# Attention and MLP block on one core: whole products and five exp banks in the half cycles after the last max product

## The chip, the cores and the metric

The kernel runs on one core of a Trainium2 chip. The metric is the device time of one execution in microseconds (us), the median of several runs. A profile of one execution is read beside it. The engines are called as in the profile: PE (TensorE, the matmul array; PEld is its weight load), DVE (VectorE), ACT (ScalarE), POOL (GpSimd), SP (SyncE, which issues the transfers).

## What is computed

One block with an adaptive layer norm: attention with 32 query heads of width 16 over one shared key and value head, then a two-layer MLP, on 2048 rows of width 512, in float32.

```python
mod = (_silu(c) @ w_mod).reshape(c.shape[0], 6, 1, -1)
sa, ca, ga, sb, cb, gb = (mod[:, 0], ..., mod[:, 5])
h = _layernorm(x, axis=-1) * (1 + ca) + sa
q = (h @ wq).reshape(B, S, 32, 16).transpose(0, 2, 1, 3)
k, v = h @ wk, h @ wv
p = _softmax(jnp.einsum("bhqd,bkd->bhqk", q, k) * 16 ** -0.5)
x = x + ga * (jnp.einsum("bhqk,bkd->bhqd", p, v) ... @ wo)
h = _layernorm(x, axis=-1) * (1 + cb) + sb
x = x + gb * (_gelu(h @ w1 + b1) @ w2 + b2)
```

## The kernel before

Products are made in float32 accuracy out of two rounded parts: each operand is split into a high and a low part, and one product becomes three (high x high, low x high, high x low).

**Units, steps, half cycles.** The queries are cut in eight blocks of 256 rows; a unit is one block with four heads, so there are 64 units (`units`, line 462), and eight steps in each (`steps`, line 1305), a step being two key tiles of 128. The main loop (lines 1350 to 1448) takes two steps at a time, X = K and Y = K + 1, and does them as two half cycles. A half cycle issues, on PE:

- four **exp products** (`sexp`, line 590), scores of a key tile against a unit's queries. They contract only 64 rows, so two of them, called s = 0 and s = 1, lie on the two halves of the array. Each fills a PSUM bank named e; ACT reads the bank with an exp (line 611) into the tile p.
- **max products** (`Max.step`, line 498, banks of tag m): the same scores in another order for a unit several units ahead; DVE reduces each to a maximum (line 510), which is later put in as a row of the queries by `put_max` (POOL line 553, SP line 548). They run ahead, so they end before the loop does. The last unit's last max product belongs to the first pair of steps of the last unit but one.
- a **batch** of the MLP's or a projection's products (`take`, line 1169; the lists come from `batches`, line 167). Such products contract 128 rows. In the loop each is done as two halves of 64 rows (`half`, line 187; `halves`, line 1374): the first half beside exp products on the other half of the array, the second in the next half cycle.
- the **pv step** (`pv`, line 619, line 628): the exps of an earlier half cycle times the values, summed in acc.

**Banks.** PSUM has three e banks, three of tag m, one each of tags x and v. `sexp` takes the e banks in turn from the list `banks` (line 586).

**Order.** The order of the instructions on every engine is that in which the program issues them; `issue` (line 1320) merges lists of products by their lengths. When a batch is there, `beside` and `follow` hold the exp of one exp product back until another, of the other half of the array, has been issued. Delayed work is put in a list with `later`, counted in ticks of `clock`, four to a pair of steps; each tick of the tail takes one batch.

**The end.** While the last block is in attention, the MLP of the block before it (number 6) is in its second product, w2: two tiles of 33 products each (`rest_steps`, lines 1015 to 1027). The batch of the first tile is `BATCH - 1` = 5 long, of the second 6; `batches` counts them from the end, so that the first batch is the short one. What isn't issued when the loop ends is issued whole (`whole`, line 179, line 181) in the tail, lines 1452 to 1466. There the last block's rest runs with `fast`: 18 products wops, then `TAIL[0]` = 4 ticks, six products wops that need the last unit's normalised result (onH, onL), `TAIL[1]` = 8 ticks, then transposes tp, w1 and w2 of the last block.

Of the kernel before, what the change touches and what calls it, by code (L numbers as in the profile page):

```python
# [8 lines left out]
F32 = mybir.dt.float32  # L9
# [5 lines left out]
P = 128  # L15
# [18 lines left out]
BATCH = 6  # L34
# [16 lines left out]
def adaln_mqa_mlp(  # L51
# [99 lines left out]
    def due():  # L151
        now = [p for p in pending if p[0] <= clock[0]]
        pending[:] = [p for p in pending if p[0] > clock[0]]
        for _, fn in now:
            fn()
# [11 lines left out]
    def batches(ps, pairs, size, ready=lambda n: True, begin=True, end=True):  # L167

        todo = [(a, b_) for wh, wl, xh, xl in pairs for a, b_ in ((wh, xh), (wl, xh), (wh, xl))]
        last = len(todo) - 1  # L170

        ends = list(range(len(todo), 0, -size))[::-1]
        for begin_, end_ in zip([0] + ends, ends):
            part = range(begin_, end_)
            while not ready(part[-1] // 3):
                yield -1
            yield [(ps, *todo[n], begin and n == 0, end and n == last) for n in part]

    def whole(batch):
        for ps, a, b_, first_, last_ in batch:  # L180
            nc.tensor.matmul(ps, a, b_, start=first_, stop=last_)  # L181
# [408 lines left out]
    def sexp(u, K, j, s, line=None):  # L590

        w = blocks[units[u][0]][1]
        qst = qsts[u]
        assert u in placed
        n = u * steps[0] + K
        if n < 3 and n not in pbufs:
            pbufs[n] = att.tile([P, 2, 2, 512], F32, name=f"p{n}", tag="p", bufs=3)
        pt = pbufs[n % 3]
        bank = banks.pop(0)
        banks.append(bank)  # L600
        e = psum.tile([P, 512], F32, name=f"e{u}_{K}_{j}_{s}", tag=f"e{bank}", bufs=1)
        rows = slice(64 * s, 64 * s + 64)
        if w == 512:
            kt, rhs = K, qst[rows, j, :]
        else:
            kt, rhs = 2 * K + j, qst[rows].rearrange("p j n -> p (j n)")
        nc.tensor.matmul(e, ks[rows, kt * P:(kt + 1) * P], rhs, start=True, stop=True)  # L607
        dst = pt[:, j, s, :]

        def exp():  # L610
            ins = nc.scalar.activation(dst, e, AF.Exp, scale=0.25)  # L611
            for old in written.pop((n - 3, j, s), ()):
                tc.declare_no_dep(ins.ins, old, reason="the products that read the tile's last contents come between the two")
            written.setdefault((n, j, s), []).append(ins.ins.name)
            return ins

        return exp() if line is None else line.append(exp)
# [190 lines left out]
    def rest_steps(b, fast, rp, bank, ons, ready):  # L808
# [4 lines left out]
        for hf in range(w // HQ):  # L813
# [201 lines left out]
            for t in range(2):  # L1015
                sl = slice(t * P, (t + 1) * P)
                for cols in (slice(0, D), ):
                    place = dict(tag="m", bufs=3) if b == len(blocks) - 2 and t else bank()
                    ps = psum.tile([P, D], F32, name=f"w2ps{b}_{hf}_{t}_{cols.start}", **place)
                    ops = [(gH[:, f, sl], gL[:, f, sl], w2H[:, f, cols], w2L[:, f, cols]) for f in range(NF)]  # L1020
                    size_ = BATCH - 1 if b == len(blocks) - 2 and not t else BATCH
                    yield from batches(ps[:, :cols.stop - cols.start], ops, size_, lambda f: made.issuperset(range(f + 1)))
                    if fast:
                        later(1, lambda t=t, ps=ps, cols=cols: store(t, ps, cols))
                        yield 2
                    else:
                        store(t, ps)
# [126 lines left out]
    def resume():  # L1154

        go_on(holder[0])
# [190 lines left out]

    keep_warm(WARM[3], tag="e2", bufs=1)
    behind = None
    for u in range(NU):  # L1350
        for K in range(0, steps[u], 2):
            goal = lead[u] + (lead[u + 1] - lead[u]) * (K + 2) / steps[u]
            goal = min(goal, first[u + QBUFS] if u + QBUFS < NU else first[NU])
            n = max(0, 2 * round((goal - mp.done) / 2))

            def maxes(s, n, first_=1.0, held=None):
                return [(1.0 if i else first_, lambda i=i: mp.step(s, held if i >= 2 else None)) if mp.has(s) else (0.0, lambda: None)
                        for i in range(n)]

            def exps(s, which):  # L1360
                return [(1.0, lambda K=K, j=j: sexp(u, K, j, s)) for K, j in which]

            def beside(s, which):

                K, j = which[-1]
                return exps(s, which[:-1]) + [(1.0, lambda: sexp(u, K, j, s, waiting))]

            def follow(s, K, j):

                state["witness"] = sexp(u, K, j, s)  # L1370
                while waiting:
                    waiting.pop()()

            def halves(batch, s):

                ahead = (SHORT if short else AHEAD) / products(batch)
                behind_ = None if s == 0 and batch[0][3] else state["witness"]
                return [(ahead * products([one]), lambda i=i, one=one: half(one, s, None if i else behind_))
                        for i, one in enumerate(batch)]

            def plain(s, K, t, n):

                one, other = maxes(s, n), maxes(t, n)
                if not holder and mp.has(t) and n > 1:

                    other[0] = 1.0, lambda: mp.step(t, tag="x", bufs=1)
                issue(mixture(exps(s, [(K, 0), (K, 1)]), one), exps(t, [(K, 0)]) + other + exps(t, [(K, 1)]))

            X, Y = K, K + 1

            due()
            batch = take() if behind else None
            short = batch and products(batch) < SHORT + 0.01
            if short:
                issue(mixture(maxes(1, n // 2), exps(1, [(X, 0), (X, 1)])),
                      exps(0, [(X, 0)]) + halves(batch, 0) + [(1.0, lambda: follow(0, X, 1))])
            elif batch:
                groups = [mixture(maxes(1, n // 2, 0.01), beside(1, [(X, 0), (X, 1), (Y, 0)])),  # L1400
                          halves(batch, 0) + [(1.0, lambda: follow(0, X, 0))]]
                issue(*(reversed(groups) if batch[0][3] else groups))
            else:
                plain(1, X, 0, (n + 2) // 4)
            clock[0] += 1
            due()
            if behind:
                end_step(*behind)
            clock[0] += 1
            due()  # L1410
            if batch:

                reduces, gone = [], []

                def hold(reduce):
                    reduce() if gone else reduces.append(reduce)

                def go_on_():
                    resume()
                    gone.append(True)  # L1420
                    while reduces:
                        reduces.pop(0)()

                hold = hold if batch[-1][4] else None

                if short:
                    issue(mixture(maxes(0, n // 2, held=hold), exps(0, [(Y, 0), (Y, 1)])),
                          exps(1, [(Y, 0)]) + halves(batch, 1) + [(0.0, go_on_), (1.0, lambda: follow(1, Y, 1))])
                else:
                    issue(mixture(maxes(0, n // 2, 0.01, hold), beside(0, [(X, 1), (Y, 0), (Y, 1)])),  # L1430
                          halves(batch, 1) + [(0.0, go_on_), (1.0, lambda: follow(1, Y, 1))])
                advance()
            else:
                plain(1, Y, 0, n // 4)
            clock[0] += 1
            due()
            end_step(u, X)
            behind = (u, Y)
            clock[0] += 1
            if state["mods"] and state["q"] == 0 and w2H is None:  # L1440
                w2H = att.tile([P, NF, D], F32R, name="w2H", tag="bigH")
                w2L = att.tile([P, NF, D], F32R, name="w2L", tag="bigL")
                preps["w2"] = prep_w2()
            if clock[0] >= prepared[0] + PREP and weights and weights[0] in preps and not state["busy"]:
                prepared[0] = clock[0]
                for _ in range(state["turns"]):
                    if weights and next(preps[weights[0]], 0) == 0:
                        weights.pop(0)
# [51 lines left out]
```

## Time and profile before

| | us |
|---|---|
| median of 3 runs | 1564.13 (1564.03 to 1564.39) |
| span of the profiled execution | 1563.1 |
| busy: PE | 1546.5 |
| busy: DVE | 1401.7 |
| busy: ACT | 1228.8 |
| busy: POOL | 681.7 |

The span runs from the first instruction to the last of the profiled execution; its own time is that span, and the runs' median is 1.0 us longer. Busy time of PE counts an array that has any product in flight as busy, even if only one half of it is used, and the ends of products are modelled. So PE's share says little about how well it is filled: the starts of products, seen in the timeline, say more. "64*128" in a row is the part of the array in use (rows x columns), 64x512 the operand. A bracket behind a row is the idle time of the engine before it and what ended it.

### The profile page before, as it was taken

The page shows a single profiled execution, that of the slowest core. Times are in us where ns is not written, and L with a number is a line of the kernel's source. Part 1 is how long each engine was busy: PE and PEld are TensorE (multiplying, and loading weights), DVE is VectorE, ACT ScalarE, POOL GpSimd, SP SyncE. Part 2 cuts the span into 40 slices and gives each one's busy share as a digit, 9 for nine tenths or more (in the row PEclk, how much of TensorE's full clock was granted, in tenths as well). Part 3 has the DMA queues.
Part 4 walks back from the last instruction along what each step waited for, and adds up shares of the span by engine and source line. Part 5 has one row for each costly group of instructions (what it writes and reads, how often), then busy time and mean ns, then how long its engine had stood idle before and what let it go on. Part 6 is the DMA issues. An engine that isn't in the chain of part 4 may idle for free.

```text
span 1563.1 us, 41433 instructions
## 1 busy us (share of the span) xinstructions
PE 1546.5 (99%) x16387; PEld 959.9 (61%) x16387; DVE 1401.7 (90%) x2479; ACT 1228.8 (79%) x2392; POOL 681.7 (44%) x1194
## 2 busy tenths in 40 slices
PE   7999999999999999999999999999999999999999
PEld 4455555567655665557655675556655676556667
DVE  7999999999999999999999999999999999999625
ACT  5577778788777887788877887788877888788853
POOL 5545433877323570246422472245611573235711
PEclk9999999999999999999999999999999999999999
DMA  7235412313030211213022120303112130312241
GB/s 244 97 96 194 152 52 89 120 52 97 19 110 19 83 60 35 93 29 99 29 62 69 57 84 26 105 16 97 43 50 79 46 97 20 102 34 66 81 150 61
DMA packets 83126, 121.63 MB, mean 78 GB/s; under 512 B 19614, under 2 KB 56222, under 8 KB 82676
## 3 DMA queue, kind: packets, MB, share of 16 engines
q1 hardware_dynamic: 82916, 118.97, 23.5%
q8 instruction: 130, 2.13, 0.6%
q14 instruction: 64, 0.52, 0.1%
q10 hardware_dynamic: 16, 0.00, 0.0%
HBM read 91.13 MB, written 27.27 MB: 76 GB/s over the span
## 4 chain that ended last, share of the span: by engine, by line
PE 84%; DVE 10%; issue 3%; POOL 2%; DMA 1%; ACT 0%; ACTq 0%; SPq 0%; POOLq 0%; DVEq 0%
PE acc L628 28%; PE m L505 24%; PE e L607 16%; DVE mx L510 8%; PE w1ps L191 8%; PE w2ps L181 2%; PE w2ps L191 1%; PE w1ps L181 1%; DMA xt<-in_A_x_dram 1%; PE qps L191 1%; PE tp L191 1%; PE wops L191 1%; PE kps L162 1%; DVE st L835 1%; DVE x L828 1%
## 5 line engine op out<-in xcount | busy, mean ns | idle before, releaser
L510 DVE TENSOR_REDUCE mx<-m 128x1 f32<-128x512 f32 x2048 | 1270.5, 682 | 86.9 <-PE m L505 63.8
L611 ACT ACTIVATE p<-e 128x512 f32<-128x512 f32 x2048 | 1099.3, 598 | 257.4 <-PE e L607 110.5
L505 PE MATMUL m<-ks,qst 64*128 64x512 f32 x2048 | 832.4, 429 | 1.9 <-DVE mx L510 0.6
L607 PE MATMUL e<-qst,ks 64*128 64x512 f32 x2048 | 747.6, 412 | 0.1
L628 PE MATMUL acc<-p,va 128*32 128x256 f32 x8192 | 548.0, 385 | 0.0
L505 PEld LDWEIGHTS m<-ks,qst 64*128 64x128 f32 x2048 | 366.5, 184 | 212.3 <-DVE mx L510 174.8
L607 PEld LDWEIGHTS e<-qst,ks 64*128 64x128 f32 x2048 | 362.5, 184 | 95.2 <-ACT p L611 71.1
L628 PEld LDWEIGHTS acc<-p,va 128*32 128x32 f32 x8192 | 213.7, 109 | 213.1 <-issue 110.0
L553 POOL TENSOR_SCALAR mt<-turned 8x32 f32<-8x32 f32 x256 | 53.1, 208 | 418.9 <-DVE turned L559 406.9
L191 PE MATMUL w1ps<-h2H,w1t 64*128 64x256 f32 x1232 | 235.6, 287 | 0.0
L191 PEld LDWEIGHTS w1ps<-h2H,w1t 64*128 64x128 f32 x1232 | 185.8, 184 | 28.9 <-DVE mx L510 17.7
L191 PE MATMUL w1ps<-h2L,w1t 64*128 64x256 f32 x616 | 169.2, 275 | 0.0
L191 PE MATMUL w2ps<-w2H,gH 64*128 64x512 f32 x284 | 123.8, 436 | 0.0
L191 PEld LDWEIGHTS w1ps<-h2L,w1t 64*128 64x128 f32 x616 | 114.0, 185 | 0.0
L191 PE MATMUL w2ps<-w2L,gH 64*128 64x512 f32 x282 | 110.9, 393 | 0.0
L191 PE MATMUL w2ps<-w2H,gL 64*128 64x512 f32 x282 | 110.2, 391 | 0.0
L954 POOL TENSOR_SCALAR tt<-tt 128x256 f32<-128x256 f32 x77 | 31.0, 403 | 142.6 <-ACT tt L953 109.3
L137 POOL TENSOR_TENSOR gL<-z,gH 128x256 fp32r<-128x256 f32 x77 | 57.0, 740 | 6.4
L955 POOL TENSOR_TENSOR tt<-tt,z 128x256 f32<-128x256 f32 x77 | 56.7, 736 | 6.4
L965 POOL TENSOR_TENSOR z<-tt,z 128x256 f32<-128x256 f32 x77 | 56.4, 733 | 6.0
L964 POOL TENSOR_TENSOR tt<-tt,z 128x256 f32<-128x256 f32 x77 | 56.4, 732 | 0.0
L191 PEld LDWEIGHTS w2ps<-w2H,gL 64*128 64x128 f32 x282 | 52.2, 185 | 0.4
(190 smaller groups left out, 1480.9 us busy)
## 6 DMA issues: line engine op xcount, KB each, us to landing
w1t<-dw SPq DMA_DIRECT2D x82, 512.0 KB
qst<-dq SPq DMA_DIRECT2D x384, 32.0 KB
do<-oc SPq DMA_DIRECT2D x64, 128.0 KB
dw<-w1s SPq DMA_DIRECT2D x11, 512.0 KB
xt<-in_A_x_dram SPq DMA_DIRECT2D x4, 1024.0 KB
dq<-qH SPq DMA_DIRECT2D x16, 256.0 KB
dq<-qL SPq DMA_DIRECT2D x16, 256.0 KB
x<-in_A_x_dram SPq DMA_DIRECT2D x8, 512.0 KB
```

Source lines behind the costliest of these rows:

```text
L137: eng_l.tensor_tensor(out=dst_l, in0=src, in1=raw(dst_h), op=ALU.subtract)
L181: nc.tensor.matmul(ps, a, b_, start=first_, stop=last_)
L191: ins = nc.tensor.matmul(ps, a[rows], b_[rows], start=first_ and s == 0, stop=last_ and s == 1)
L505: nc.tensor.matmul(m, qsts[u][rows, j, t * P:(t + 1) * P], ks[rows, kc * 512:(kc + 1) * 512], start=True, stop=True)
L510: nc.vector.tensor_reduce(out=self.mx[u][:, i, kc:kc + 1], in_=m, axis=AX.X, op=ALU.max)
L553: nc.gpsimd.tensor_scalar(out=mt[:, g:g + 32], in0=turned[g:g + 4 * T, :], scalar1=1.0, scalar2=0.0, op0=ALU.mult, op1=ALU.add)
L607: nc.tensor.matmul(e, ks[rows, kt * P:(kt + 1) * P], rhs, start=True, stop=True)
L611: ins = nc.scalar.activation(dst, e, AF.Exp, scale=0.25)
L628: ins = nc.tensor.matmul(accs[u][32 * cidx:32 * cidx + 32, :], va[:, kt, :], rhs, start=kt == 0, stop=kt == NKT - 1)
L955: nc.gpsimd.tensor_tensor(out=tt, in0=tt, in1=z, op=ALU.mult)
L964: nc.gpsimd.tensor_tensor(out=tt, in0=tt, in1=z, op=ALU.mult)
L965: nc.gpsimd.tensor_tensor(out=z, in0=tt, in1=z, op=ALU.add)
```

## The change

After the last max product the loop takes another path. `bare` is set at the first pair of steps at which no max product is left. Then two more banks, of tag m, are put in front of the list `banks`, and stay in it, so that exp products go round five banks. `alone` does a half cycle: the four exp products of a step in the order (s = 0, s = 1, s = 0, s = 1), then half of the batch's products as whole ones of 128 rows. No exp is held back. Such half cycles are those of steps 2 to 7 of the last unit but one, and all of the last unit. In them the rest of the loop (the pv steps, the ticks, the work at their ends) is as before.

The first w2 tile of block 6 is cut in batches of `SHORT` = 4 in place of 5, and `batches` joins a first batch of one product to the next one, so that the tile's batches are 5, 4, 4, 4, 4, 4, 4, 4 long in place of 3, 5, 5, 5, 5, 5, 5. No other list of products has a first batch of one.

```diff
@@ batches
         ends = list(range(len(todo), 0, -size))[::-1]
+        if ends[0] == 1:
+            ends.pop(0)
         for begin_, end_ in zip([0] + ends, ends):
@@ sexp
         bank = banks.pop(0)
         banks.append(bank)
-        e = psum.tile([P, 512], F32, name=f"e{u}_{K}_{j}_{s}", tag=f"e{bank}", bufs=1)
+        if not isinstance(bank, int):
+            e = bank
+        else:
+            e = psum.tile([P, 512], F32, name=f"e{u}_{K}_{j}_{s}", tag=f"e{bank}", bufs=1)
@@ rest_steps
-                    size_ = BATCH - 1 if b == len(blocks) - 2 and not t else BATCH
+                    size_ = SHORT if b == len(blocks) - 2 and not t else BATCH
@@ main loop
+    bare = [False]
...
+            if not bare[0] and not mp.has(0) and not mp.has(1):
+                bare[0] = True
+                banks[:0] = [psum.tile([P, 512], F32, name=f"e_{i}", tag="m", bufs=3) for i in range(2)]
+
+            def alone(K, part):
+                issue(exps(0, [(K, 0), (K, 1)]), exps(1, [(K, 0), (K, 1)]))
+                whole(part)
+
             due()
             batch = take() if behind else None
             short = batch and products(batch) < SHORT + 0.01
-            if short:
+            if bare[0]:
+                alone(X, batch[:len(batch) // 2] if batch else [])
+            elif short:
...
             due()
-            if batch:
+            if bare[0]:
+                alone(Y, batch[len(batch) // 2:] if batch else [])
+                if batch:
+                    resume()
+                    advance()
+            elif batch:
```

## The prediction

> **What bounds the kernel now.** I read the page first: the span, and who holds the chain of work that ended last.
>
> ```profile
> span 1563.1 us, 41433 instructions
> ...
> PE 84%; DVE 10%; issue 3%; POOL 2%; DMA 1%; ACT 0%; ACTq 0%; SPq 0%; POOLq 0%; DVEq 0%
> ```
>
> TensorE (PE) sets the end nearly everywhere. The edits act only after the last max product, so next I read the chain in order of time for the end of the span: start, duration, work.
>
> ```profile
> 1471.28 1.00 PE acc L628 x16
> ...
> 1474.08 1.00 PE acc L628 x16
> ...
> 1476.88 1.00 PE acc L628 x16
> ...
> 1479.49 1.00 PE acc L628 x16
> ...
> 1508.32 1.86 PE acc L628 x32
> 1510.18 4.37 PE wops L181 x18
> 1514.55 4.59 PE w2ps L181 x20
> 1519.14 1.89 PE wops L181 x6
> 1521.04 4.13 PE w2ps L181 x18
> 1525.17 0.44 PE tp L912 x4
> ```
>
> Each acc entry is one pv step (L628), one per half cycle. The acc at 1471.28 follows the last max product; from its start to that of the acc at 1508.32 there are fourteen half cycles without max products and 37.04 us. The first two, with w1 products, last 2.80 us each (1471.28 to 1474.08 to 1476.88), the others 2.6 (1476.88 to 1479.49 is 2.61). Behind stands the tail of whole products.
>
> Which wait ends last inside a half cycle is in the timeline (start, duration, engine, line, idle before and releaser):
>
> ```profile
> 1497.80 1.07 PE L628 MATMUL acc<-p,va 128*32 128x256 f32 x16
> 1498.80 0.50 PE L607 MATMUL e<-qst,ks 64*128 64x512 f32 x1
> 1498.80 0.50 PE L191 MATMUL w2ps<-w2H,gH 64*128 64x512 f32 x1
> ...
> 1499.14 0.40 PE L607 MATMUL e<-qst,ks 64*128 64x512 f32 x1
> 1499.14 0.39 PE L191 MATMUL w2ps<-w2H,gL 64*128 64x512 f32 x1
> ...
> 1499.33 2.27 ACT L611 ACTIVATE p<-e 128x512 f32<-128x512 f32 x4 [0.34 <-PE w2ps L191]
> 1499.37 0.39 PE L191 MATMUL w2ps<-w2L,gH 64*128 64x512 f32 x1
> ...
> 1499.38 0.39 PE L607 MATMUL e<-qst,ks 64*128 64x512 f32 x1
> 1499.61 0.39 PE L191 MATMUL w2ps<-w2H,gH 64*128 64x512 f32 x1
> ...
> 1499.83 0.39 PE L191 MATMUL w2ps<-w2H,gL 64*128 64x512 f32 x1
> 1499.98 0.18 PEld L607 LDWEIGHTS e<-qst,ks 64*128 64x128 f32 x1 [0.19 <-ACT p L611]
> 1500.07 0.42 PE L607 MATMUL e<-qst,ks 64*128 64x512 f32 x1
> 1500.41 0.59 PEld L628 LDWEIGHTS acc<-p,va 128*32 128x32 f32 x16 [0.25 <-issue]
> ```
>
> The two halves of the array run side by side in slots: starts at 1498.80, 1499.14, 1499.37, 1499.61, 1499.83 and 1500.07, then pv at 1500.41. Three of the six slots have one half empty: two hold a w2 half alone, and the last an exp product (e) that could not start earlier because its bank was being read (0.19 us of waiting on ACT). ACT idles 0.34 us before its first exp. So it is a closed ring, pv, first e, first exp, the e that needs its bank, pv, and the slots in it are badly filled. A full slot costs 0.23 us (1499.14 to 1499.37); the first after pv 0.34, the last before pv 0.34 (1500.07 to 1500.41).
>
> **The change, part by part.** The instruction order as built moves nothing on DVE, POOL and SP. It differs on PE and ACT alone, from the acc at 1471.28 on.
>
> *Bank and order of the exp products.* Two banks of tag m join the three e banks, and a half cycle issues its four e products as two pairs, one of each array half. That two e take one slot is seen at the loop's start:
>
> ```profile
> 74.85 0.56 PE L607 MATMUL e<-qst,ks 64*128 64x512 f32 x2
> 75.19 0.80 PE L505 MATMUL m<-ks,qst 64*128 64x512 f32 x2
> ```
>
> Two e hold 0.34 us there. With five banks the fourth e of a half cycle needs the bank of the third exp of the half cycle before, so the ring opens. ACT then needs, back to back:
>
> ```profile
> 1480.96 2.07 ACT L611 ACTIVATE p<-e 128x512 f32<-128x512 f32 x4 [0.25 <-PE e L607]
> ```
>
> Four exps in 2.07, one alone being 0.60 long, make (2.07 - 0.60) / 3 = 0.49 per exp, 1.96 per half cycle.
>
> *Whole products.* Two w2 products of 128 rows (half of a batch of four) replace five half products. Six slots become four: two e pairs and two whole products. But the array now changes shape three times per half cycle (pv to halves, halves to whole, whole to pv) in place of two. The price of a change stands in the prologue, where pairs of half products alternate with three whole ones:
>
> ```profile
> 47.75 0.50 PE L505 MATMUL m<-ks,qst 64*128 64x512 f32 x2
> 48.17 0.50 PE L162 MATMUL kps<-bigH,wkH 128*128 128x512 f32 x1
> 48.52 0.39 PE L162 MATMUL kps<-bigH,wkL 128*128 128x512 f32 x1
> 48.75 0.40 PE L162 MATMUL kps<-bigL,wkH 128*128 128x512 f32 x1
> 49.07 0.50 PE L505 MATMUL m<-ks,qst 64*128 64x512 f32 x2
> 49.50 0.50 PE L162 MATMUL kps<-bigH,wkH 128*128 128x512 f32 x1
> ```
>
> From 48.17 to 49.50 are 1.33 us for four slots (three whole, one pair) of 0.23: 0.41 over for two changes, 0.205 each, partly before and partly after the change. The same price fits pv: 2.61 - 6 x 0.23 - 2 x 0.205 leaves 0.82 for pv itself.
>
> This is where a rule of the Trainium skill speaks against the edit: "TensorEngine Tiling (Array Packing)", Key Properties, says that changing the tiling mode, unlike changing only the tile, drains the array. By that rule the third change is paid in full, as the prologue's 0.41 per two has it (sum below: -1.9); were only changes of tile paid for nothing and this one counted among them, the sum would be -4.8.
>
> New half cycle: 0.82 + 4 x 0.23 + 3 x 0.205 = 2.355 us, ACT's 1.96 hidden under it. With three w2 products (the second half of the first batch, five long): 2.585. The first two carry six w1 products of 256 columns each, at
>
> ```profile
> 1527.90 15.87 PE w1ps L181 x132
> ```
>
> 15.87 / 132 = 0.12: 0.82 + 2 x 0.23 + 6 x 0.12 + 3 x 0.205 = 2.615. Fourteen: 2 x 2.615 + 2.585 + 11 x 2.355 = 33.72. Gain 37.04 - 33.72 = **3.32 us**.
>
> The unknown in it is the third change, which this kernel never makes between an e and a w2 product. Bounds: nothing (14 x 0.205 = 2.87 more gain), and the 0.41 of a pair of changes on it alone (2.87 less gain). I take 0.205, as m products have the shape of e products and kps that of whole w2 ones.
>
> *What starts the stage.* The new banks must be free of max products, and ACT still has gelu work in its queue:
>
> ```profile
> 1471.55 1.28 DVE L510 TENSOR_REDUCE mx<-m 128x1 f32<-128x512 f32 x2
> ...
> 1479.16 0.73 POOL L955 TENSOR_TENSOR tt<-tt,z 128x256 f32<-128x256 f32 x1
> ...
> 1482.25 0.57 SPq L548 DMA_DIRECT2D qst<-ml  x1
> ```
>
> Of the last two reductions the earlier ends near 1472.2, when the first e comes up; the bank under the later is not taken. The last tanh waits in ACT's order behind the e_4 exps for POOL's 1479.16 + 0.73 = 1479.9; by the sums above these exps end near 1480.0, so it costs nothing, but a stage 0.5 us faster would have ACT, and the e behind it, wait there. The last unit's maxima leave SP at 1482.25 to 1482.8; its first e comes at 1472.3 + 2 x 2.615 + 2.585 + 3 x 2.355 = 1487.2: over 4 us for the transfer, no wait.
>
> *Batches of four.* The first w2 tile is cut 5, 4, 4... in place of 3, 5, 5.... Up to the end of the loop 25 products are issued instead of 28; 41 stay for the tail instead of 38. They fill two holes there, in ticks of one batch: 20 and 18 before (rows above), 17 and 24 after. The first hole is ended by a chain that starts from the last pv, not by PE:
>
> ```profile
> 1519.13 0.19 PEld L181 LDWEIGHTS wops<-woH,onH 128*128 128x128 f32 x1 [0.42 <-ACT onH L132]
> ...
> 1525.02 0.55 DVE L847 TENSOR_SCALAR xh<-x,mv,rs 128x512 f32<-128x512 f32 x1 [0.46 <-POOL rs L844]
> ```
>
> Three products fewer there only lengthen PE's wait for onH by 0.69 us. The second hole is full: tp follows the last w2 product, and the second xh (ready at 1525.57) is needed only by the second tp group, later than that. Six products more cost 6 x 0.23 = **1.38 us**. Bounds: 0.69 (three more products in all, if the first hole became shorter too) and 1.38; I take 1.38.
>
> **Sum.** -3.32 + 1.38 = -1.94 us: span 1563.1 to 1561.2. The runs shown have a median 1.0 above that span (1564.13), so **1562.2 us**.
>
> **Rivals.**
> - *The third change of shape is free* (or hidden under the weight load). Gain 2.87 more: 1564.13 - 4.81 = 1559.3. For it: the loads run ahead of the products; against it: the prologue rows, where they do as well and 0.41 is paid.
> - *ScalarE becomes the bound.* If exps don't overlap, four cost 4 x 0.60 = 2.40 per half cycle against 2.355: 14 x 0.045 = 0.6 lost, 1562.8. For it: 2.27 for four in the rows of 1499.33; against: that includes a wait, and the 2.07.
> - *Exp products queue up, slower.* An e behind a bank that ACT still reads stops everything behind it on PE, both whole products and pv, and exps of the next half cycle come late in turn. Its place is the third and fourth e. If each took a slot for itself, as the last e does now, a half cycle costs 2 x 0.23 more: 14 x 0.46 = 6.4, 1568.6. The result is slower than before from 1.94 / 14 = 0.14 us of such waiting per half cycle on. For it: that 0.19 us wait exists today; against: two banks more, and the exp waited for then ends about half a microsecond before its bank is needed.
> - That nothing changes is out: the order differs for fourteen half cycles.
>
> **How the numbers follow.** Forecast 0.58, its own range 1560.6 to 1563.7 (the first pair of bounds taken half way); free change 0.22; ScalarE 0.10; queueing 0.10. A measurement of this kernel is taken to tell 0.2%, 3.1 us, from no change. Faster by more (under 1561.0): the free change, and 0.05 of the forecast's lower edge, 0.27. Slower (over 1567.3): most of the queueing, 0.07. Within: 0.66. The range must reach the free change: 1559.2 to 1564.7; queueing lies outside.
>
> **What would show it.** Right: e in pairs, pv starts 2.35 to 2.4 us apart, slots of about 0.33 on both sides of the pass from e to w2, no PE wait on ACT in the loop, tail holes of 17 and 24 with PE waiting about 1.1 us on onH. The forecast is wrong if pv starts lie 2.15 apart (free change), if PE waits for ACT on e or pv (ScalarE, queueing), or if the tail from the last pv to the first tp, 16.85 us from 1508.32 to 1525.17, grows by other than 1.4.

## The result and the profile after

| | before | after |
|---|---|---|
| median of 20 runs, us | 1564.20 (1563.25 to 1565.55) | 1561.89 (1560.98 to 1564.64) |
| span of the profiled execution, us | 1563.1 | 1560.1 |

The ratio is 0.9984, with a 95% interval of 0.9978 to 0.9991: 2.3 us less, 1.4 to 3.4. Forecast were 1562.2 us and 1.9 us less. The two profiled executions lie 3.0 us apart, more than the medians, so the stages are compared with each other below rather than the spans. In every run for which both are listed, the time is 1.7 to 1.9 us above its own span, and five runs of the kernel before with a span of 1563.1 us took 1564.9. So the page of before shows an execution of about 1564.9 us (an estimate), 0.7 above the median: the 1.0 us between span and median, given with the time before, compares two executions. The forecast, 1.94 less than the median, does not hang on it.

The chain that ended last in the changed kernel, in order of time (start, duration, work):

```profile
1471.17 1.00 PE acc L633 x16
1472.17 0.74 PE e L612 x4
1472.90 0.89 PE w1ps L183 x6
1473.80 1.00 PE acc L633 x16
...
1495.22 1.00 PE acc L633 x16
1496.22 0.67 PE e L612 x4
1496.89 0.66 PE w2ps L183 x2
1497.55 1.00 PE acc L633 x16
...
1504.51 1.92 PE acc L633 x32
...
1510.39 3.42 DMA os_last<-dr
...
1514.85 1.89 PE wops L183 x6
1516.74 5.51 PE w2ps L183 x24
1522.25 0.44 PE tp L917 x4
```

The fourteen half cycles from 1471.17 to 1504.51 take 33.34 us, where they took 37.04. One with two w2 products is 0.67 for two e pairs, 0.66 for two whole products and 1.00 for pv, 2.33 us in all. From the last pv to the first tp are 17.74 us instead of 16.85. Before the stage (-0.11) and after it (37.93 to 37.85, -0.08) nothing moved: -0.11 - 3.70 + 0.89 - 0.08 = -3.0, the difference of the spans.

One half cycle in the timeline of the changed kernel (start, duration, engine, line, idle before and releaser):

```profile
1491.48 0.30 PEld L612 LDWEIGHTS e<-qst,ks 64*128 64x128 f32 x4 [0.41 <-issue]
1491.49 0.74 PE L612 MATMUL e<-qst,ks 64*128 64x512 f32 x4
1492.03 2.06 ACT L616 ACTIVATE p<-e 128x512 f32<-128x512 f32 x4 [0.27 <-PE e L612]
1492.15 0.19 PEld L183 LDWEIGHTS w2ps<-w2H,gL 128*128 128x128 f32 x1 [0.37 <-issue]
1492.15 0.50 PE L183 MATMUL w2ps<-w2H,gL 128*128 128x512 f32 x1
...
1492.49 0.40 PE L183 MATMUL w2ps<-w2L,gH 128*128 128x512 f32 x1
1492.82 0.59 PEld L633 LDWEIGHTS acc<-p,va 128*32 128x32 f32 x16 [0.37 <-issue]
```

All four e products go in one piece, and none waits for a bank, here and in the other thirteen half cycles. ACT waits for PE (0.27 us), no longer PE for ACT. The weight load sits idle about 0.4 us at each of the three changes of shape of this half cycle, and no semaphore ends that idle time ("issue").

### The profile page after: what moved, and what is told of

Read it like the earlier page. It is cut to its first block, busy times and chain, and to the rows that moved or that the text cites. A ratio compares the mean times of both kernels' runs of the same rounds, so it can differ in the third digit from the quotient of the medians.

```text
span 1560.1 us, 41350 instructions
## 1 busy us (share of the span) xinstructions
PE 1543.2 (99%) x16347; PEld 955.2 (61%) x16347; DVE 1400.8 (90%) x2479; ACT 1227.4 (79%) x2392; POOL 681.5 (44%) x1194
## 4 chain that ended last, share of the span: by engine, by line
PE 84%; DVE 10%; issue 3%; POOL 2%; DMA 1%; ACT 1%; SPq 0%; POOLq 0%; DVEq 0%
PE acc L633 28%; PE m L507 24%; PE e L612 15%; DVE mx L512 8%; PE w1ps L193 8%; PE w2ps L183 2%; PE w1ps L183 1%; DMA xt<-in_A_x_dram 1%; PE w2ps L193 1%; PE qps L193 1%; PE tp L193 1%; PE wops L193 1%; PE kps L162 1%; DVE st L840 1%; DVE x L833 1%
## 5 line engine op out<-in xcount | busy, mean ns | idle before, releaser
L612 PE MATMUL e<-qst,ks 64*128 64x512 f32 x2048 | 739.9, 413 | 0.0
L612 PEld LDWEIGHTS e<-qst,ks 64*128 64x128 f32 x2048 | 358.7, 185 | 92.3 <-ACT p L616 64.0
L193 PE MATMUL w2ps<-w2H,gH 64*128 64x512 f32 x264 | 115.9, 439 | 0.0
L193 PE MATMUL w2ps<-w2L,gH 64*128 64x512 f32 x264 | 103.4, 392 | 0.0
L193 PE MATMUL w2ps<-w2H,gL 64*128 64x512 f32 x264 | 103.0, 390 | 0.0
L193 PE MATMUL wops<-woH,onH 64*128 64x512 f32 x112 | 49.8, 444 | 0.0
```

What stands on the lines that cost most here:

```text
L193: ins = nc.tensor.matmul(ps, a[rows], b_[rows], start=first_ and s == 0, stop=last_ and s == 1)
```

## Experiments

None of the kernels leaves out or changes part of the computation. The time to the start of the stage differs by up to 4 us between profiled executions of the same instructions, so the table counts from the start of the pv step behind the last max product. "Loop" is from there to the last half cycle's pv, "tail" from that pv to the first tp, "rest" from the beginning of the stage to the end of the span, all read from the timelines (whose starts lie a few hundredths beside those of the chain). The ratio is that of the runs to those of the kernel before.

| kernel | loop | tail | rest | ratio (95%) |
|---|---|---|---|---|
| before | 37.04 | 16.76 | 91.89 | 1 |
| changed | 33.34 | 17.65 | 89.00 | 0.9984 (0.9978 to 0.9991) |
| changed, again | 33.35 | 17.27 | 88.65 | 0.9981 (0.9972 to 0.9990) |
| five | 34.03 | 16.26 | 88.29 | 0.9974 (0.9963 to 0.9984) |
| five, again | 34.03 | 16.26 | 88.29 | 0.9975 (0.9966 to 0.9984) |
| four | 37.23 | 17.63 | 93.07 | 1.0007 (0.9998 to 1.0016) |
| split | 38.89 | 17.26 | 94.17 | 1.0014 (1.0005 to 1.0023) |
| three_banks | 46.60 | 17.30 | 101.90 | 1.0060 (1.0042 to 1.0078) |
| none | 28.99 | 21.05 | 90.60 | 0.9997 (0.9988 to 1.0006) |
| tail5 | 33.32 | 16.97 | 88.43 | 0.9980 (0.9971 to 0.9989) |
| alternate | 33.74 | 17.93 | 89.76 | 0.9991 (0.9982 to 1.0000) |
| alt_tail5 | 33.76 | 16.94 | 88.84 | 0.9984 (0.9976 to 0.9993) |
| alternate6 | 32.36 | 17.23 | 87.82 | 0.9974 (0.9965 to 0.9984) |
| best | 32.98 | 16.25 | 87.34 | 0.9970 (0.9958 to 0.9982) |

**The two parts of the change, each alone.** *five* keeps the half cycles and takes the batches back; *four* keeps the batches and never enters the new path:

```diff
 five:
-                    size_ = SHORT if b == len(blocks) - 2 and not t else BATCH
+                    size_ = BATCH - 1 if b == len(blocks) - 2 and not t else BATCH
 four:
-            if not bare[0] and not mp.has(0) and not mp.has(1):
+            if False:
```

> The new half cycles with the old batches of five (3, 5, 5, ...). Theory (slots of 0.23 us, three changes of shape per half cycle): three more w2 products in the loop, +0.7 us there, and the tail's holes back at 20 and 18, -0.9 to -1.4 us: 0.2 to 0.7 us faster than the changed kernel, about 1561.4 us; pv starts 2.33 us apart with two products, 2.56 with three. Rival (the smaller batches shorten the loop): pv starts back at 2.5 to 2.6 us everywhere, 1563.5 us or more.

> The batches of four alone, half cycles and three banks as before. Theory: the ring of pv, e, exp and the e that waits for its bank keeps half cycles at 2.6 us; the tail's holes are 17 and 24 and cost 0.9 to 1.4 us: 1565.1 to 1565.6 us against 1564.2 before, slower than both kernels. Rival (batch size makes the gain): 2.4 us or less per half cycle, 1562 us or less.

Measured: five takes 0.7 us less than the changed kernel from the stage's start to the end (88.29 against 89.00; 0.4 less than its second profile, 88.65), with half cycles of 2.33 and 2.56 us. Four takes 1.2 us more than before, with most half cycles at 2.61. In four the batches are short enough for the old loop's `short` branch, which issues the products in another order than before; its half cycles have six slots all the same, and the load for the last e waits 0.19 us for ACT (at 1495.57). So the half cycles make the whole gain, and the batches of four take part of it back: they save 0.7 us in the loop and add 1.0 to 1.4 in the tail. The five kernel's tail shows why:

```profile
1505.81 1.86 PE acc L633 x32
1507.68 4.36 PE wops L183 x18
1512.04 4.59 PE w2ps L183 x20
1516.63 1.40 PE wops L183 x6
1518.03 4.13 PE w2ps L183 x18
1522.16 0.44 PE tp L917 x4
```

The six wops products take 1.40 us, without a wait, against 1.89 and 1.69 in the two profiles of the changed kernel: with 20 products ahead of them PE arrives 0.4 us after onL is ready (0.1 us after in the second profile of five). The kernel before has the same 20 and 18 products and did wait for onH (0.42 us); its profile drew a long transfer, as shown further below. The second run of five, beside the changed kernel on one chip, gave the same loop, tail and rest. The ratios of the two kernels overlap; the stages of the profiles part them.

**The price of a change of shape.** *split* puts the whole products in two places, behind each e pair:

```diff
-                issue(exps(0, [(K, 0), (K, 1)]), exps(1, [(K, 0), (K, 1)]))
-                whole(part)
+                issue(exps(0, [(K, 0)]), exps(1, [(K, 0)]))
+                whole(part[:len(part) // 2])
+                issue(exps(0, [(K, 1)]), exps(1, [(K, 1)]))
+                whole(part[len(part) // 2:])
```

> The changed kernel with the whole products put one part behind each e pair: five changes of shape per half cycle instead of three, the same products. Theory (0.205 us a change): 14 x 0.41 = 5.7 us slower than the changed kernel, 1567.6 us, pv starts 2.74 us apart. Rival (a change between halves and whole is free): 1561.9 us, 2.33 us apart.

The chain of split, one half cycle:

```profile
1493.55 1.00 PE acc L633 x16
1494.55 0.44 PE e L612 x2
1494.99 0.43 PE w2ps L183
1495.42 0.43 PE e L612 x2
1495.85 0.43 PE w2ps L183
1496.28 1.00 PE acc L633 x16
```

The same four slots take 1.73 us instead of 1.33: 0.40 for two more changes. Over the loop it is 38.89 - 33.34 = 5.55 us for 28 changes, 0.198 us each. The rival that a change between halves and whole is free falls.

**The banks.** *three_banks* leaves the two added banks out:

```diff
-                banks[:0] = [psum.tile([P, 512], F32, name=f"e_{i}", tag="m", bufs=3) for i in range(2)]
```

> The changed kernel without the two added banks. Theory: the fourth e of a half cycle waits for the first exp of the same half cycle, about 0.9 us, with the whole products and pv queued behind it: pv starts 3.2 us apart, 14 x 0.88 = 12 us slower, about 1574 us. Rival (the order and the whole products make the gain, banks do not matter): 1561.9 us.

Its timeline:

```profile
1492.00 0.73 PE L612 MATMUL e<-qst,ks 64*128 64x512 f32 x3
1492.54 2.06 ACT L616 ACTIVATE p<-e 128x512 f32<-128x512 f32 x4 [1.22 <-PE e L612]
1493.19 0.18 PEld L612 LDWEIGHTS e<-qst,ks 64*128 64x128 f32 x1 [0.89 <-ACT p L616]
...
1493.62 0.50 PE L183 MATMUL w2ps<-w2H,gH 128*128 128x512 f32 x1
```

The fourth e waits 0.89 us for the first exp, with both whole products and pv behind it; half cycles take 3.28 us, the loop 13.3 us more. This is the queueing that the prediction gave as the slower rival: it is real, and the two banks take it away.

What the whole products add by themselves is not shown: no kernel here gives the added banks to half cycles of half products. With the four e on one half of the array beside five w2 halves on the other, the prediction's prices give 0.82 + 5 x 0.23 + 2 x 0.205 = 2.38 us (an estimate), 4.76 for two half cycles, where five takes 4.89 for the same products. So it is open whether the gain needed the whole products, or only the banks and another order.

**Where ACT becomes the bound.** *none* takes no w2 batch in the last twelve half cycles:

```diff
-            batch = take() if behind else None
+            batch = take() if behind and (not bare[0] or (u, K) < (NU - 2, 4)) else None
```

> The changed kernel with no w2 products in the last twelve half cycles; all 66 stand in the tail. Theory: PE then needs 0.82 + 2 x 0.23 + 2 x 0.205 = 1.69 us and ACT 4 x 0.49 = 1.96 us a half cycle, so ACT sets it: 12 x 0.37 + 0.2 = 4.7 us less in the loop, 25 x 0.23 = 5.8 us more in the tail, 1563.0 us. Rival (exps do not overlap, ACT needs 2.40 us): the loop does not get shorter, 1568 us. Rival (PE alone sets it): 1.69 us, 1559.8 us.

Its chain:

```profile
1492.72 1.00 PE acc L633 x16
1493.72 0.96 PE e L612 x3
1494.68 1.00 PE acc L633 x16
```

Half cycles of 1.96 us, where PE needs 1.67 (the short half cycles of alternate below), in long stretches: four exps at 0.49. (Two take 2.3 us, one around the copy of the finished unit on ACT, the other around a tanh there.) So ACT's floor is 0.37 us below the changed kernel's half cycle and does not bind there. The whole came out 1.6 us longer than the changed kernel (90.60 to 89.00), where 1.1 was expected: the loop is 4.35 us shorter, and what follows it 5.95 longer, about the 25 x 0.23 = 5.75 of the products moved there. The loop without them runs into ACT, so it can't give that back.

**The tail.** *tail5* gives the first hole one batch more:

```diff
-TAIL = (4, 8)
+TAIL = (5, 8)
```

> The changed kernel with one tick more ahead of the last wops products: holes of 23 and 18 in place of 17 and 24. Theory (the first hole is ended by the chain from the last pv to onH, the second by PE): six products less in the second, -1.4 us; the first hole overruns the chain by 1.0 us, of which the wait for onL gives back 0.5: 0.8 us faster than the changed kernel, 1561.1 us. Rival (only the number of products in the tail counts): no change, 1561.9 us.

The tail is 16.97 us, 0.3 to 0.7 less than in the two profiles of the changed kernel. In time the two kernels can't be told apart (0.9980 against 0.9984 and 0.9981). The mechanism holds (six wops products, no wait), its worth is below what the runs resolve.

**Fewer changes of shape.** *alternate* puts a batch's products into every second half cycle; *alt_tail5* adds the tail's edit:

```diff
-                alone(X, batch[:len(batch) // 2] if batch else [])
+                alone(X, [])
...
-                alone(Y, batch[len(batch) // 2:] if batch else [])
+                alone(Y, batch or [])
```

> The changed kernel with all of a batch's whole products in every second half cycle and none in the others: per pair of half cycles five changes of shape in place of six. Theory: 7 x 0.205 = 1.4 us faster, 1560.5 us, less up to 1.0 us if the fourth e of a long half cycle meets an exp that is still running (then 1561.5 us); a short half cycle takes about 1.7 us, a long one 2.8. Rival (the change is free): 1561.9 us.

> Both edits, the products in every second half cycle and holes of 23 and 18. Theory: the two gains add, 1559.7 to 1560.7 us.

Alternate missed: its loop takes 33.74 us, 0.4 more than the changed kernel's, where 0.4 to 1.4 less was expected; alt_tail5 likewise 33.76. The timeline of alternate has the wait that its expectation named as the risk:

```profile
1493.07 1.00 PE L612 MATMUL e<-qst,ks 64*128 64x512 f32 x4
1493.56 0.18 PEld L612 LDWEIGHTS e<-qst,ks 64*128 64x128 f32 x1 [0.20 <-ACT p L616]
```

A short half cycle is over before ACT has done its exps, so that the fourth e of the long one meets a running exp. A long half cycle takes 3.06 us. *alternate6* gives the loop a sixth bank, the third of tag m, and *best* takes batches of five besides:

```diff
-                banks[:0] = [psum.tile([P, 512], F32, name=f"e_{i}", tag="m", bufs=3) for i in range(2)]
+                banks[:0] = [psum.tile([P, 512], F32, name=f"e_{i}", tag="m", bufs=3) for i in range(3)]
```

> Whole products in every second half cycle, with six banks (all three of tag m). Theory (the fourth e of a long half cycle met a running exp, which cost 0.26 us in each): with six banks it needs the second exp of the half cycle before, the wait goes, long half cycles fall from 3.06 to 2.80 us, short ones stay at 1.67: 4.47 per pair against 4.65 in the changed kernel, about 1.2 us faster than it over seven pairs, 87.8 us from the last max product's pv start to the end. Rival (something else makes the long half cycles long): 3.06 us, 89.8 us.

> The same with batches of five, so that the tail's holes are 20 and 18. Theory: short half cycles 1.67 us, long ones 3.03 with five products, 4.70 per pair against 4.88 in the kernel with batches of five alone: about 1.2 us faster than that, 87.1 us from the last max product's pv start to the end, 1559.5 us on the scale of 1564.2 before. Rival (ACT has no room for an uneven half cycle): no gain over it, 88.3 us.

> The changed kernel once more, beside the next three on the same chip: 2.3 us faster than before, as measured. From the last max product's pv start to the end of the span 89.0 us, as in its first profile, within 0.4 (the chain of transfers to onH varies by that).

> The new half cycles with batches of five once more, beside the changed kernel on the same chip: theory 0.7 us faster than that, 88.3 us from the last max product's pv start to the end; a difference from the changed kernel that is absent here would make the earlier one chance.

The chain of best, one pair of half cycles:

```profile
1490.08 1.00 PE acc L633 x16
1491.09 0.66 PE e L612 x4
1491.74 1.00 PE acc L633 x16
1492.74 0.66 PE e L612 x4
1493.40 1.35 PE w2ps L183 x5
1494.76 1.00 PE acc L633 x16
```

The pair takes 4.68 us with five products, against 4.89 in five; the long half cycle of alternate6, with four, falls from 3.06 to 2.78 to 2.80, so the bank was the cause. From the stage's start to the end best needs 87.34 us, 0.95 less than five (1.2 was expected), 1.66 and 1.31 less than the two profiles of the changed kernel, 4.55 less than before. Its median was 1560.14 us beside 1561.73 of the changed kernel, 1561.26 of five and 1564.64 of the kernel before: the fastest of all, though the intervals of the ratios overlap.

## Why the prediction held

*What bound the kernel* was right: the ring of pv, first e, first exp and the e that needs its bank, with slots half empty. With the batches alone (four) most half cycles stay at 2.61 us; with the ring open they take 2.33, and no e waits for ACT.

*The half cycle* was forecast at 2.355 us and measured at 2.33. The loop fell by 3.70 us where 3.32 were forecast. The term that was too high is pv with the change behind it: 0.82 + 0.205 = 1.025 us in the sum, 1.00 in the chains of both kernels, which makes 14 x 0.025 = 0.35 of the missing 0.38. The 0.82 was what remained of an old half cycle of 2.61 us behind six slots and two changes; that it was all pv was not shown. The change of shape itself was priced well: two pairs, two whole products and the two changes behind them take 0.67 + 0.66 = 1.33 us, as the four slots of the prologue do, and split has 0.198 us for the 0.205.

The rule of the Trainium skill ("TensorEngine Tiling (Array Packing)", Key Properties: a change of tiling mode drains the array) fits these numbers: the third change is paid, not hidden under weight loads. What goes on in the array meanwhile no trace here shows.

*The cover of ACT*: 1.96 us worked out, 1.96 measured in none. *The banks*: 0.9 us of waiting per half cycle without them, as three_banks has it.

*The tail* was forecast at +1.38 us and measured at +0.89 and +0.51 in the two profiles of the changed kernel. By the prediction's own sign, a growth other than 1.4, this step failed. The holes are 17 and 24 as read, and the second costs six products. But the chain to onH was taken as fixed from one execution. The kernel before:

```profile
1514.18 0.61 SPq L664 DMA_DIRECT2D os_last<-dr  x1
...
1518.21 0.43 DVE L666 TENSOR_TENSOR os_last<-os_last 128x256 f32<-128x256 f32 x1 [1.78 <-DMA os_last<-dr]
```

The changed kernel:

```profile
1513.94 0.43 DVE L671 TENSOR_TENSOR os_last<-os_last 128x256 f32<-128x256 f32 x1 [0.60 <-DMA os_last<-dr]
...
1514.85 0.18 PEld L183 LDWEIGHTS wops<-woH,onH 128*128 128x128 f32 x1 [0.61 <-ACT onH L132]
```

From the last pv's start to the issue of the transfer from dr it is 5.93 us before, 5.95 and 5.96 in the changed kernel. From there to the operation on DVE that waits for it, it is 4.03 us before (1514.18 to 1518.21), but 3.55 (1510.39 to 1513.94) and 3.16 in the changed kernel. Five, with the same instructions in its two profiles, has 3.04 and 3.40; tail5 has 4.00. So the difference belongs to the execution and not to the change, and the profile of before has the longest transfer of all. PE's wait for onH was 0.6 and 0.2 us, not 1.1. Against five, whose wops do not wait, the tail grows by 1.39 and 1.01 us.

Both errors have one sign: in the profiles 3.0 us less than before, from 1.94 forecast. In the medians it is 2.3, which the 3.70 measured in the loop and the 1.38 forecast for the tail would also give; the medians' interval of 1.4 to 3.4 can't decide that. So the forecast is not near by errors that cancel. *The rivals*: the free change fell with split, ScalarE as the bound with none; queueing was shown, in the kernel without the banks.

## What to carry to other kernels

Count slots and changes of the array's shape before sharing the array between half products and whole ones: a slot of 512 columns is 0.23 us here and a change 0.2, so by these prices a whole product beside a half one pays only if the slots saved outnumber the changes added. The ring of matmul, evacuation and matmul was opened here by banks (3.28 us a half cycle with three, 2.33 with five); how many are needed follows from which earlier read each product waits for: five for even half cycles, six for uneven ones. Work moved into a tail should be cut so that each wait there is just filled: tail5, with 23 products in the first hole for the 20 of five, has a tail longer by the three (0.71 us), and the changed kernel, with 17, got back at most 0.4 of the 0.69 us of the three that it leaves out there.

## What was not expected of the hardware

The transfer from dr at the end, with the same instructions, took between 3.04 and 4.03 us from its issue to the operation that waits for it in the fourteen profiles, and that difference is more than some edits here are worth. And the 1471 us ahead of the stage, with the same instructions in all kernels, took between 1470.7 and 1472.1 us in most profiled executions, and 1474.4 and 1475.0 in two whose mean granted clock was 0.998 (tail5 and alternate6), where 0.2% of 1471 us is 2.9:

```profile
core 0: 1562.8 us, clock 0.998
```

That is why single spans mislead here: alternate6 has a span of 1562.8 us against the changed kernel's 1560.1, and the shorter times in the runs (1560.72 against 1561.73 us, beside each other).
